# An attention-and-MLP kernel whose static order is planned anew: a policy per stretch, two more result buffers, another first stage

## The chip, the cores and the metric

The kernel runs on one core of one Trainium2 chip. The metric is the device time of one execution in microseconds (us). Before the change it is 673.41 us, the median of three runs (673.37 to 673.63). Engines are named as the profile names them: PE is the matmul engine and PEld its weight loads, ACT the engine of activation functions, DVE the vector engine, POOL the engine beside it, SP the one that issues most DMAs.

## The reference

The input is x of 2048 rows by 512 columns. It is normalized by rows, xn. Two branches read xn and are added to x: attention with 32 heads of 16, and a token-mixing MLP, which normalizes once more and multiplies along the rows.

```python
def _A_ref(x, wqkv, wo):
    H = 32; Dh = D // H
    qkv = (x @ wqkv).reshape(B, S, 3, H, Dh).transpose(2, 0, 3, 1, 4)
    q, k, v = qkv[0], qkv[1], qkv[2]
    scores = jnp.einsum("bhqd,bhkd->bhqk", q, k) * Dh ** -0.5
    p = _softmax(scores, axis=-1)
    o = jnp.einsum("bhqk,bhkd->bhqd", p, v)
    return o.transpose(0, 2, 1, 3).reshape(B, S, D) @ wo

def _B_ref(x, w1, b1, w2, b2):
    h = _layernorm(x, axis=-1)
    u = _gelu(jnp.einsum("bsd,sf->bdf", h, w1) + b1)
    y = jnp.einsum("bdf,fs->bds", u, w2) + b2
    return y.transpose(0, 2, 1)

xn = _layernorm(A_x, axis=-1)
return A_x + _A_ref(xn, A_wqkv, A_wo) + _B_ref(xn, B_w1, B_b1, B_w2, B_b2)
```

Most of the work is the softmax numerator: 32 heads x 2048 x 2048 exponentials.

## The kernel before

**Tiling.** Attention goes in 32 blocks: 4 blocks of 512 queries times 8 groups of 4 heads. In each block the keys go in 16 tiles of 128, so there are 512 groups of one key tile, four heads and 512 queries. A group has four score tiles of 128 x 512 (`score_mm`, L590), one PSUM bank each; the four matmuls use different rows of PE. PSUM has eight banks: 0 to 3 are two pairs for ACT, 6 gathers the products of the block (PV), and 4, 5 and 7 serve everything else.

**Two ways to an exponential.** A group goes to ACT or to the vector side.

- ACT: two exponentials of 128 x 1024 (`exp_tile`, L598), each reading a pair of banks and writing one of eight buffers of the tile pT. PV (`pv_mm`, L610) then needs one set of four matmuls for the group.
- Vector side: the exponential is approximated by writing bit patterns. DVE turns each score bank into 16-bit integers (`dve_first`, L657; `dve_first2` takes two banks at once), which read as bfloat16 are a rough power of two. Two more "planes", the same integers plus a shift, correct it: made by DVE (`add_plane`, L670) or by POOL (`add_plane_pool`, L677). All three planes are multiplied with V, so PV needs three sets of four matmuls. Planes are put wherever memory is free: in the tiles plx, x_sb, xn_sb, h_sb, w1blk, wqkv_sb and xnT once their first contents are done with.

**The first stage** loads x, normalizes the first four row tiles (statistics on DVE at L462 and L466, epsilon and power at L478 and L480 on POOL, the normalization on ACT at L487 for tile 0 and on DVE at L496 for the others), transposes them over PE (L692), copies them to xnT and makes the first Q and K (`qt0_mm`, `k_mm`, L531; `qt_evac`, L551; `k_evac`, L527). After it a dispatcher takes over.

**The order.** All instructions are written out in Python by a planner, class `Sched`: each operation has a planned duration, `add` computes its start from what it depends on, and a loop of `pe_step`, `dve_step` and `misc_step` picks the next operation of each engine at the planned time. On the chip each engine only follows its written order, in order, and waits on semaphores. When ACT's pair of banks is free by the plan, `pe_step` issues two scores for it and one exponential (L598), and as many scores for the vector side as banks are free; otherwise `pe_fill` puts in PV sets or steps of other chains: Q, K and V of later heads (L531), the MLP's two products (L924 and L955, with the Gelu on ACT at L946 between them), the output product (L965). A plan-time rule keeps DVE's planes behind a running POOL plane (`wide`); a POOL operation waits on the chip for the DVE plane ahead of it (`two`).

The choices are steered by 16 numbers, `POLICY`, for instance the lateness that PE may bring to ACT (TOL), when POOL takes a plane (POOL_MIN), when DVE's planes go ahead of its first copies (PL_PRI), and a seed for small variations (SEED). They can differ for each stretch of 10 us of planned time (SEG); before, one row holds for all.

Of the kernel before, what the change touches and what calls it, by code (L numbers as in the profile page):

```python
# [11 lines left out]
F32 = mybir.dt.float32  # L12
# [47 lines left out]
NPB = 8  # L60
NQS = 4
# [34 lines left out]
POLICY = [(150.0, 200.0, 450.0, -1, 0, 1300.0, 0.0, 0.05, 2, 3, 2, 7500.0, 0, 0.0, 1100.0, 0)]  # L96
# [3 lines left out]
POOL_PLANE = 2350.0  # L100
# [173 lines left out]
def bass_parallel_sum__softmax_full_mha__mixer_token_mlp__prompt_kernel(  # L274
# [18 lines left out]
    with ExitStack() as es:  # L293
# [41 lines left out]
        mhalf = sb("mhalf", [128, NT], F32)  # L335
        shift_w = sb("shift_w", [128, NPL], I32)
# [47 lines left out]
        sc.add("pool", lambda e: e.memset(mhalf[:], -0.5), writes=[("mhalf",)], occ=60, lat=130)  # L384
        v17_views = []
# [42 lines left out]
        ld_x(4, 6, 4500)  # L428
        ld_w(2, 0, 1, 5000, "sp")
        ld_x(6, 8, 5500)  # L430
        ld_x(8, 12, 9500)
        ld_x(12, 16, 12500)
# [40 lines left out]
        def ln_stats2(t):  # L473
            if t == NPRE - 1:
# [9 lines left out]
        def ln_norm_act(t):  # L484
            sc.add("pool", lambda e: e.tensor_scalar(r2[:, t:t + 1], mv[:, t, 0:1], mv[:, t, 2:3], -1.0, ALU.mult, ALU.mult),
                   reads=[("mv", t), ("mvr", t)], writes=[("r2",)], occ=230, lat=310)
            return sc.add("act", lambda e: e.activation(xn_sb[:, t, :], x_sb[:, t, :], ACTF.Identity, bias=r2[:, t:t + 1],  # L487
# [99 lines left out]
        def score_mm(g, r, bk, last):  # L587
# [6 lines left out]
                reads=[("KTt", T, kt), ("QT", slot_q), ("QTr", slot_q, r)] + ([("QTh", b)] if b < 2 else []), writes=[("bank", bk)], name="sc",  # L594
                occ=(222.0 if last else 4.0), lat=430.0, cfg="S")

        def exp_tile(slot, buf):
            return sc.add("act", lambda e: e.activation(pT[:, buf, :], ps[:, slot * 1024:(slot + 1) * 1024],  # L598
                                                        ACTF.Exp, scale=EXP_SCALE),
                          reads=[("bank", 2 * slot), ("bank", 2 * slot + 1)], writes=[("pT", buf)], name="exp",  # L600
                          occ=917.0, lat=1080.0)
# [30 lines left out]
        for reg, nm in ((x_flat, "x"), (xn_flat, "xn")):  # L632
            for j in range(4):
# [109 lines left out]
        ln_norm_act(0)  # L743
        ln_stats(1)
# [9 lines left out]
        qt0_mm(0, QB)  # L754
        k_mm(0, KB, 0)
# [1248 lines left out]
```

## Time and profile before

| what | value |
|---|---|
| median of three runs | 673.41 us |
| profiled execution | 673.31 us |
| its span, first to last instruction | 671.5 us |
| ACT busy | 658.0 us, 98% |
| PE busy | 643.1 us, 96% |
| DVE busy | 615.8 us, 92% |
| POOL busy | 355.6 us, 53% |
| exponentials on ACT | 700 |
| PE clock granted | 1.000 |

A line of the profile's groups has the source line, engine and operation, what it writes and reads with the shape, the count, the busy time and the mean duration in ns, then the idle time before it and what ended it. In the timeline a line has its start and its length in us and how many equal instructions follow each other. Busy matmuls are pipelined, so PE's share is not its load.

### The profile page before, as it was taken

To read this page: it belongs to the slowest core of one execution; us is meant where nothing else is said; L and a number is where in the kernel's file an instruction comes from. 1 tells how busy PE (TensorE), PEld (TensorE's weight loads), DVE (VectorE), ACT (ScalarE), POOL (GpSimd) and SP (SyncE) were. 2 spreads that over 40 slices of the span, in tenths; PEclk is the share of its full clock that TensorE was granted. 3 is DMA by queue.
4 is the path that set the end of the run, shared out by engine and by line. 5 is a ranking of instruction groups with operands and counts; after the bars stand their busy time and mean duration, and the time that the engine had idled before them with its cause. 6 is when DMAs were issued, how large, how long until landed. Compare 5 with 4: busy or idle time off the path is not lost.

```text
span 671.5 us, 15513 instructions
## 1 busy us (share of the span) xinstructions
PE 643.1 (96%) x6272; PEld 196.0 (29%) x6348; DVE 615.8 (92%) x1066; ACT 658.0 (98%) x716; POOL 355.6 (53%) x254
## 2 busy tenths in 40 slices
PE   8999999999999999999999999999998999999997
PEld 4533333322222222222222222222222222222222
DVE  7888999999999998999999899999999988999996
ACT  6999999999999999999999999999999999999996
POOL 5620665356465466446655445565645666455570
PEclk9999999999999999999999999999999999999999
DMA  7142100122212222210022121221120222222001
GB/s 220 33 83 42 34 16 17 26 52 51 54 25 44 50 57 53 52 37 19 27 61 53 45 51 45 56 50 34 47 59 20 58 62 49 58 55 52 26 22 48
DMA packets 78368, 32.67 MB, mean 49 GB/s; under 512 B 63004, under 2 KB 74204, under 8 KB 78296
## 3 DMA queue, kind: packets, MB, share of 16 engines
q1 hardware_dynamic: 77864, 31.27, 19.5%
q8 instruction: 50, 0.82, 0.5%
q10 hardware_dynamic: 432, 0.39, 0.2%
q14 instruction: 22, 0.18, 0.1%
HBM read 26.08 MB, written 2.61 MB: 43 GB/s over the span
## 4 chain that ended last, share of the span: by engine, by line
PE 60%; ACT 31%; DVE 6%; issue 1%; DMA 1%; POOL 0%; DVEq 0%
ACT pT L598 30%; PE ps L590 22%; PE ps L610 22%; PE ps L924 6%; PE ps L531 5%; PE ps L955 3%; PE ps L965 1%; DVE plx L657 1%; DVE xn_sb L657 1%; ACT gT L946 1%; DVE x_sb L657 1%; DVE stats L462 1%; DMA den_s<-den_scr 0%; PE ps L692 0%; DVE KT L527 0%
## 5 line engine op out<-in xcount | busy, mean ns | idle before, releaser
L598 ACT ACTIVATE pT<-ps 128x1024 bf16<-128x1024 f32 x700 | 644.1, 1117 | 2.1 <-PE ps L590 1.4
L590 PE MATMUL ps<-QT,KT 32*128 32x512 bf16 x2048 | 283.7, 384 | 10.0 <-ACT pT L598 7.0
L590 PEld LDWEIGHTS ps<-QT,KT 32*128 32x128 bf16 x2048 | 73.8, 91 | 266.5 <-ACT pT L598 245.7
L610 PE MATMUL ps<-pT,V 128*32 128x512 bf16 x1400 | 137.9, 390 | 1.6 <-issue 0.5
L657 DVE TENSOR_SCALAR xn_sb<-ps 128x512 int16<-128x512 f32 x160 | 105.7, 683 | 11.7 <-PE ps L590 10.2
L657 DVE TENSOR_SCALAR x_sb<-ps 128x512 int16<-128x512 f32 x160 | 106.7, 684 | 9.8 <-PE ps L590 8.1
L657 DVE TENSOR_SCALAR plx<-ps 128x512 int16<-128x512 f32 x116 | 76.7, 683 | 6.2 <-PE ps L590 5.9
L610 PEld LDWEIGHTS ps<-pT,V 128*32 128x32 bf16 x1400 | 35.4, 93 | 77.6 <-issue 71.1
L657 DVE TENSOR_SCALAR wqkv_sb<-ps 128x512 int16<-128x512 f32 x80 | 52.8, 684 | 4.0 <-PE ps L590 3.6
L677 POOL TENSOR_TENSOR x_sb<-xn_sb,shift_w 128x1024 int32<-128x1024 int32 x14 | 26.5, 1891 | 51.1 <-DVE x_sb L670 32.7
L924 PE MATMUL ps<-h_sb,w1blk 128*128 128x512 bf16 (+1 forms) x161 | 50.6, 386 | 2.4 <-issue 2.4
L955 PE MATMUL ps<-gT,w2blk 128*128 128x512 bf16 (+1 forms) x151 | 48.9, 384 | 3.3 <-issue 3.2
L531 PE MATMUL ps<-xnT,wqkv_sb 128*128 128x512 bf16 (+1 forms) x166 | 36.0, 305 | 3.8 <-issue 2.7
L657 DVE TENSOR_SCALAR w1blk<-ps 128x512 int16<-128x512 f32 x48 | 31.8, 683 | 2.9 <-PE ps L590 2.3
L610 PE MATMUL ps<-xn_sb,V 128*32 128x512 bf16 x344 | 33.0, 382 | 0.1
L1213 POOL TENSOR_TENSOR oT<-OT,denb 128x512 bf16<-128x512 f32 x16 | 20.3, 1271 | 23.4 <-DVE xn_sb L670 9.4
L657 DVE TENSOR_SCALAR xnT<-ps 128x512 int16<-128x512 f32 x44 | 29.2, 685 | 3.4 <-PE ps L590 3.3
L610 PE MATMUL ps<-x_sb,V 128*32 128x512 bf16 x328 | 31.5, 383 | 0.0
L657 DVE TENSOR_SCALAR h_sb<-ps 128x512 int16<-128x512 f32 x40 | 26.3, 684 | 2.2 <-PE ps L590 2.0
L1213 POOL TENSOR_TENSOR otmp<-OT,denb 128x512 bf16<-128x512 f32 x15 | 19.1, 1271 | 11.5 <-DVE x_sb L670 5.7
L677 POOL TENSOR_TENSOR x_sb<-plx,shift_w 128x1024 int32<-128x1024 int32 x9 | 17.0, 1891 | 14.2 <-DVE x_sb L670 4.4
L677 POOL TENSOR_TENSOR xn_sb<-plx,shift_w 128x1024 int32<-128x1024 int32 x9 | 17.0, 1891 | 12.2 <-DVE xnT L670 4.9
(184 smaller groups left out, 802.7 us busy)
## 6 DMA issues: line engine op xcount, KB each, us to landing
denb<-rec_scr SPq DMA_DIRECT2D x124, 64.0 KB, 2.1
w1blk<-in_B_w_dram SPq DMA_DIRECT2D x10, 512.0 KB, 4.1
w2blk<-in_B_w_dram SPq DMA_DIRECT2D x16, 320.0 KB, 3.4
xres<-in_A_x_dram SPq DMA_DIRECT2D x16, 128.0 KB, 2.9
QT<-qst SPq DMA_DIRECT2D x120, 16.0 KB, 1.8
out_dram<-osb SPq DMA_DIRECT2D x14, 128.0 KB, 1.7
wqkv_sb<-in_A_wqkv_dram SPq DMA_DIRECT2D x3, 384.0 KB, 8.6
x_sb<-in_A_x_dram SPq DMA_DIRECT2D x2, 512.0 KB, 7.9
```

What stands on the lines that cost most here:

```text
L462: return sc.add("dve", lambda e: e.bn_stats(stats[:, t, :], x_sb[:, t, :]), reads=[("x", t)], writes=[("stats", t)], occ=620, lat=725)
L531: return sc.add("pe", lambda e: e.matmul(dst, lhsT=lhsT, rhs=rhs, start=(ct == 0), stop=(ct == NCT - 1)), reads=reads, writes=[("bank", bk ...
L590: return sc.add("pe", lambda e: e.matmul(bank(bk), lhsT=KT[32 * r:32 * r + 32, T, 128 * kt:128 * (kt + 1)], rhs=QT[32 * r:32 * r + 32, slo ...
L598: return sc.add("act", lambda e: e.activation(pT[:, buf, :], ps[:, slot * 1024:(slot + 1) * 1024], ACTF.Exp, scale=EXP_SCALE), reads=[("ba ...
L610: return sc.add("pe", lambda e: e.matmul(bank(PV_BANK)[32 * r:32 * r + 32, :], lhsT=vt_[:, off:off + 32], rhs=rhs, start=start, stop=stop, ...
L657: return sc.add("dve", lambda e: e.tensor_scalar(plane_i[pb][:, 512 * r:512 * (r + 1)], bank(bk), BIAS, 0.0, ALU.add, ALU.max), reads=[("b ...
L677: return sc.add("pool", lambda e: e.tensor_tensor(plane_w[pb], plane_w[pb0], shift_w[:, j:j + 1].broadcast_to([128, 1024]), ALU.add), read ...
L924: op = sc.add("pe", lambda e: e.matmul(bank(xb)[0:m, :], lhsT=w1blk[:, slot, st, 0:m], rhs=h_sb[:, st, :], start=(st == 0), stop=(st == NT ...
L946: op = sc.add("act", lambda e, m=m, f0=f0, f1=f1: e.activation(gT[0:m, f0:f1, :], gT[0:m, f0:f1, :], ACTF.Gelu_apprx_tanh), reads=[("gT", ...
L955: op = sc.add("pe", lambda e: e.matmul(bank(xb), lhsT=w2blk[0:m, slot, ft, :], rhs=gT[0:m, ft, :], start=first, stop=last), reads=([("w2bl ...
L965: return sc.add("pe", lambda e: e.matmul(bank(bk), lhsT=oT[:, par, T, 128 * sti:128 * (sti + 1)], rhs=wo_c[:, T, :], start=first, stop=las ...
L1213: op = sc.add("pool", lambda e: e.tensor_tensor(dst, OT32[:, eb, :], denb[:, :], ALU.mult), reads=[("OT32", eb)] + [("denb", r) for r in r ...
```

## The change

The change has these parts.

1. `POLICY` has 65 rows, one for each 10 us of planned time, for one row before.
2. `POOL_PLANE`, the planned duration of a plane on POOL, is 1888 ns for 2350.
3. ACT may write its exponentials to two further buffers besides the eight of pT (`NPX`). They lie in the last quarter of xn_sb and are used only after the second normalization has read it; one plane less is kept there.
4. In the first stage, Q of the first four tiles goes over banks 7, 4 and 5, for 7 and 4 before; Q is evacuated to QT in pieces of 256, 128 and 128 columns (before 384 and 128); K of tile 1 is made and evacuated there, so that the later chain `k1` holds tiles 2 and 3 alone, for 1 to 3 before; transposes and products of the first tiles are issued in another order; the epsilon of row tile 1 is added by ACT.
5. The planned landing times of x are shorter, and `v_ones(1)` is a step of the dispatcher.

The change was described as an order searched per stretch with three plane makers; in the instructions, planes are made by DVE and POOL before and after.

In the order that comes out, the instructions count as follows.

| instructions | before | after |
|---|---|---|
| exponentials on ACT (128 x 1024) | 700 | 690, five of them into xn_sb |
| first copies on DVE, 128 x 512 | 648 | 658 |
| first copies on DVE, 128 x 1024 | 0 | 5 |
| planes on DVE | 170 | 147 |
| planes on POOL | 154 | 187 |
| PV matmuls | 3344 | 3384 |
| score matmuls | 2048 | 2048 |
| exponentials ahead of the Gelu | 344 | 342 |

On SP, eight row transfers to QT stand ahead of the loads of wo, w1 and w2, which stood ahead of them before.

```diff
+NPX = 2
...
-POLICY = [(150.0, 200.0, 450.0, -1, 0, 1300.0, 0.0, 0.05, 2, 3, 2, 7500.0, 0, 0.0, 1100.0, 0)]
+POLICY = [
+    (160.0, 150.0, 400.0, -1, 0, 1300.0, 0.0, 0.05, 2, 3, 2, 7500.0, 0, 0.0, 1000.0, 1),
+    (115.0, 150.0, 300.0, -1, 0, 900.0, 100.0, 0.05, 2, 5, 2, 8000.0, 84539, 150.0, 1000.0, 1),
...
+]
...
-POOL_PLANE = 2350.0
+POOL_PLANE = 1888.0
...
-        ld_x(4, 6, 4500)
+        ld_x(4, 6, 4100)
...
-            if t == NPRE - 1:
+            if t == 1:
+                sc.add("act", lambda e: e.activation(mv[:, t, 3:4], mv[:, t, 1:2], ACTF.Identity, bias=epsc[:, 0:1]),
+                       reads=[("mv", t), ("epsc",)], writes=[("mve", t)], occ=150, lat=290)
+            elif t == NPRE - 1:
...
+        def pT_buf(buf):
+            return pT[:, buf, :] if buf < NPB else xn_flat[:, 8192 - 1024 * (buf - NPB + 1):8192 - 1024 * (buf - NPB)]
...
-                for j in range(4):
+                for j in range(4 if nm == "x" else 4 - NPX // 2):
...
-        ln_norm_act(0)
-        ln_stats(1)
+        ln_stats1(1)
+        ln_norm_act(0, lambda: ln_stats2(1))
...
-        qt0_mm(0, QB)
-        k_mm(0, KB, 0)
         transpose_mm(2, 0, 0)
         ln_norm(3)
         v_ones(0)
         xnT_evac(2, 1, 0, 0, "dve")
+        qt0_mm(0, QB)
+        k_mm(0, KB, 0)
+        transpose_mm(3, 1, 0)
+        k_evac(0, 1, KB, 0, "act")
+        xnT_evac(3, 1, 1, 0, "dve")
         qt0_mm(1, QB)
-        k_evac(0, 1, KB, 0, "act")
-        transpose_mm(3, 1, 0)
-        xnT_evac(3, 1, 1, 0, "dve")
-        qt0_mm(2, QB)
-        qt0_mm(3, 4)
-        qt_evac(0, QB, "act", 0, 384)
-        qt_evac(0, 4, "act", 384, 512, "QTh")
-        qt_evac(1, 4, "act", 384, 512, "QTh")
-        qt_evac(1, QB, "act", 0, 384)
+        qt_evac(0, QB, "act", 0, 256)
+        qt_evac(1, QB, "act", 0, 256)
+        qt0_mm(2, 4)
+        k_mm(1, KB, 1)
+        qt0_mm(3, 5)
+        k_evac(1, 1, KB, 1)
+        qt_evac(0, 4, "act", 256, 384, "QTh")
+        qt_evac(0, 5, "act", 384, 512, "QTi")
+        qt_evac(1, 4, "act", 256, 384, "QTh")
+        qt_evac(1, 5, "act", 384, 512, "QTi")
         ln_stats(NPRE)
         ln_stats1(NPRE + 1)
-        v_ones(1)
...
-            c = Chain("k1", [Step("pe", lambda t=t: k_mm(t, 5, t - 1), 226) for t in (1, 2, 3)]
-                      + [Step("dve", kdone, 470, frees=True)], due, -1.0, bk=[5])
+            c = Chain("k1", [Step("pe", lambda t=t: k_mm(t, 5, t - 2), 226) for t in (2, 3)]
+                      + [Step("dve", kdone, 340, frees=True)], due, -1.0, bk=[5])
...
-                free_buf = [k for k in range(NPB) if k not in buf_busy]
+                free_buf = [k for k in range(NPB if ln2_left[0] else NPB + NPX) if k not in buf_busy]
```

More of the change, by code (lines that the diff above doesn't have):

```diff
@@ L384, in bass_parallel_sum__softmax_full_mha__mixer_token_mlp__prompt_kernel @@
         sc.add("pool", lambda e: e.memset(mhalf[:], -0.5), writes=[("mhalf",)], occ=60, lat=130)
+        sc.add("pool", lambda e: e.memset(epsc[:], EPS), writes=[("epsc",)], occ=60, lat=130)
         v17_views = []
@@ L427, in bass_parallel_sum__softmax_full_mha__mixer_token_mlp__prompt_kernel @@
                occ=1500)
-        ld_x(4, 6, 4500)
+        ld_x(4, 6, 4100)
         ld_w(2, 0, 1, 5000, "sp")
-        ld_x(6, 8, 5500)
-        ld_x(8, 12, 9500)
-        ld_x(12, 16, 12500)
+        ld_x(6, 8, 4400)
+        ld_x(8, 12, 8400)
+        ld_x(12, 16, 9500)
         ld_w(1, 1, 4, 16000, "sp")
@@ L1273, in bass_parallel_sum__softmax_full_mha__mixer_token_mlp__prompt_kernel @@
             bg.append(chain_ln2(t, 1.5 + 1.0 * t / NT))
-        for i in (2, 3):
+        for i in (1, 2, 3):
             bg.append(Chain("ones%d" % i, [Step("pool", lambda i=i: v_ones(i), gate=lambda i=i: 4 * i + 1 in ln1_done)], -1.0, 0.0))
@@ L1590, in pe_fill @@
             f_first = vary(3) > 0.6
-            pv_press = len(buf_busy) >= NPB - PRESS or len(planes_avail()) < PRESS
+            pv_press = len(buf_busy) >= (NPB if ln2_left[0] else NPB + NPX) - PRESS or len(planes_avail()) < PRESS
             for c in cands:
```

26 lines of the change are left out of this document (19 added, 7 removed), and 63 rows, old and new, of the table POLICY.

## The prediction

> **What bounds the kernel now.** I read the page first: busy shares, the chain that ended last, the costliest group.
>
> ```profile
> span 671.5 us, 15513 instructions
> PE 643.1 (96%) x6272; PEld 196.0 (29%) x6348; DVE 615.8 (92%) x1066; ACT 658.0 (98%) x716; POOL 355.6 (53%) x254
> ...
> PE 60%; ACT 31%; DVE 6%; issue 1%; DMA 1%; POOL 0%; DVEq 0%
> ...
> L598 ACT ACTIVATE pT<-ps 128x1024 bf16<-128x1024 f32 x700 | 644.1, 1117 | 2.1 <-PE ps L590 1.4
> ```
>
> The page's columns: busy time, share, instructions; in the last row 644.1 us busy, 1117 ns for one, 2.1 us idle before them. Three engines look full and the chain gives PE 60%. Which of them sets the pace is told by the waits, read second:
>
> ```profile
> PEld ps L590 <- ACT pT L598: 245.7, 616, 0.8
> ```
>
> ```profile
> ACT pT L598 <- PE ps L590: 1.4, 4, 0.7
> ```
>
> The score matmuls (L590) stand 245.7 us, 616 times, until an exponential of ACT (L598) has read its two banks; ACT stands 1.4 us for the scores. So ACT is the bound from its first exponential to its last, and PE's 96% and its share of the chain are two engines handing the same path to and fro. The third view is ACT's timeline, with one stretch of the chain:
>
> ```profile
> 8.98 1.61 ACT L551 ACTIVATE QT<-ps,qmask 128x384 bf16<-128x384 f32 x4 [0.91 <-PE ps L531]
> 10.47 1.95 ACT L598 ACTIVATE pT<-ps 128x1024 bf16<-128x1024 f32 x2
> 13.06 278.76 ACT L598 ACTIVATE pT<-ps 128x1024 bf16<-128x1024 f32 x302 [0.65 <-PE ps L590]
> ...
> 328.97 1.28 ACT L946 ACT_TABLE_LOAD   x1
> ...
> 336.55 47.87 ACT L598 ACTIVATE pT<-ps 128x1024 bf16<-128x1024 f32 x52
> ...
> 386.03 278.25 ACT L598 ACTIVATE pT<-ps 128x1024 bf16<-128x1024 f32 x303 [0.39 <-PE ps L590]
> 667.29 1.08 ACT L525 ACTIVATE osb<-ps 128x512 bf16<-128x512 f32 x2 [3.01 <-PE ps L973]
> ```
>
> ```profile
> 400.90 123.88 ACT pT L598 x135
> ```
>
> An exponential takes 1.117 us, but the next starts before it ends: 135 in 123.88 us are 0.9176 us apart. The first starts at 10.47, the last ends at 386.03 + 278.25 = 664.28: 653.8 us. 700 x 0.9176 = 642.3, the Gelu with its two table loads 336.55 - 328.97 = 7.6, and 1.12 - 0.92 = 0.2 for the last one's drain make 650.1. So ACT lost 3.7 us in all. Of that, 13.06 - 10.47 - 2 x 0.918 = 0.75 lies before the third exponential. The stretch of 302 ran at (278.76 - 1.12)/301 = 0.9224, so 1.4 more. What is left, about 1.5, is spread out. Ahead lie 10.5 us, behind 671.5 - 664.3 = 7.2.
>
> The time before the first exponential plus their number at 0.9176, plus stalls, plus 7.2: this is the sum I change. The profiled execution took 673.31, of which 671.5 are span and 1.8 lie around it; the median is 673.41, so the sum made against the one moves by 0.1 to the other.
>
> **The change: the count.** The program's order has 690 exponentials after (685 into pT, 5 into xn_sb) for 700 before: five groups of keys, each two exponentials, are computed on the vector side instead (167 groups for 162). 10 x 0.9176 = **-9.18 us**, wholly on the path as long as ACT stays fed. Each gives work to others; their prices:
>
> ```profile
> 455.06 2.47 DVE L657 TENSOR_SCALAR plx<-ps 128x512 int16<-128x512 f32 x4
> ```
>
> ```profile
> L657 DVE TENSOR_SCALAR x_sb<-ps x160: 627/684/692, 85.5 to 649.8; 128x512 int16<-128x512 f32 x160
> ```
>
> ```profile
> L670 DVE TENSOR_SCALAR x_sb<-xn_sb x12: 630/683/694, 65.8 to 636.2; 128x2048 int16<-128x2048 int16 x12
> ```
>
> ```profile
> L677 POOL TENSOR_TENSOR x_sb<-xn_sb,shift_w x14: 1890/1891/1892, 66.6 to 534.1; 128x1024 int32<-128x1024 int32 x14
> ```
>
> ```profile
> 655.49 0.40 PE L610 MATMUL ps<-pT,V 128*32 128x512 bf16 x4
> ...
> 655.72 0.39 PE L610 MATMUL ps<-h_sb,V 128*32 128x512 bf16 x4
> ```
>
> - DVE: 20 more first copies of 512, (2.47 - 0.68)/3 = 0.60 us apart: +12.0. Planes fall from 170 to 147; one has the same length as a copy (0.68), so 0.60 in a row: -13.8. Five pairs of copies become one of 1024 columns, a form not seen before on this line: at worst two copies (0), at best one for two (-3.0); I take 0, the nearer row being the copy itself. DVE comes out 2 to 5 us lighter in 615.8.
> - POOL: planes rise from 154 to 187, 33 x 1.891 = +62.4, so 418 of some 661 us, 63%. It has room, and nothing waits for POOL but PV matmuls and the POOL operations behind.
> - PE: 5 groups leave five PV sets and bring fifteen: 10 more sets of four, 655.72 - 655.49 = 0.23 us each: +2.3. The 245.7 us in which PE waits for ACT hide them; were that cover gone (a set placed in a slot already full), each would put up to 0.23 on ACT.
>
> **Two more result buffers.** Only 5 of 690 exponentials use them. In the trace before no wait for a buffer shows on ACT (its waits are PE's 1.4 us), so I cost this at 0; a buffer wait that stands behind PE's late scores is part of the 1.5 us of scattered loss, which bounds the gain, and a loss is excluded but for 5 extra operands. The word "three plane makers" has no counterpart in the order: planes are made on DVE and POOL alone, as before.
>
> **The first stage.** Rows of the head:
>
> ```profile
> 5.18 0.81 ACT L487 ACTIVATE xn_sb<-x_sb,r,mv 128x512 bf16<-128x512 bf16 x1 [1.29 <-POOL r L485]
> 5.22 0.22 POOL L478 TENSOR_SCALAR mv<-mv 128x1 f32<-128x1 f32 x1
> 5.53 0.57 POOL L480 TENSOR_TENSOR mv<-mv,mhalf 128x1 f32<-128x1 f32 x1
> 6.38 1.25 POOL L480 TENSOR_TENSOR mv<-mv,mhalf 128x1 f32<-128x1 f32 x2
> 7.16 0.93 DVE L496 TENSOR_SCALAR xn_sb<-x_sb,mv 128x512 bf16<-128x512 bf16 x2 [0.46 <-POOL mv L480]
> 8.06 0.94 DVE L527 COPY xnT<-ps 128x512 bf16<-128x512 bf16 x2
> 9.91 0.39 PE L590 MATMUL ps<-QT,KT 32*128 32x512 bf16 x4 [0.46 <-ACT QT L551]
> 10.82 0.71 DVE L496 TENSOR_SCALAR xn_sb<-x_sb,mv 128x512 bf16<-128x512 bf16 x1 [0.21 <-POOL mv L480]
> 11.45 0.67 DVE L462 BATCH_NORM_STATS2 stats<-x_sb 128x6 f32<-128x512 bf16 x1
> 12.04 0.53 DVE L527 CAST KT<-ps 128x384 bf16<-128x384 f32 x1
> 12.63 0.40 PE L590 MATMUL ps<-QT,KT 32*128 32x512 bf16 x4 [0.66 <-DVE KT L527]
> ```
>
> The epsilon of row tile 1 moves from POOL (0.22 at 5.22) to ACT, into its 1.29 us of idleness ahead of the normalization, at 0. A memset of that constant is new on POOL, at most the 0.22 of a small operation there, under the same 1.29. POOL's powers follow each other, so they move up by 5.53 - 5.22 = 0.31, and DVE's norms, which wait 0.46 for them, with them. Q is evacuated in six ACT pieces over banks 7, 4 and 5 instead of four; the two wide ones no longer wait for tiles 2 and 3. That they end sooner is bounded by the 1.61 us of the four; nothing before shows the pieces, so 0 to 0.8. I take **-0.30** for the first exponential: POOL's move alone, as the Q pieces are still behind tile 3's copy (8.06 to 9.00).
>
> The third exponential waited because K tiles 1 to 3 came in one copy at 12.04, behind a norm and statistics on DVE. After, tile 1 has its own copy right behind the xnT copies, about 9.0, and tiles 2 and 3 stand two statistics later, near 11: both ahead of need. So **-0.75** (bounds 0 and -0.75). What is late next: the tiles of row 4 on, whose norms DVE delivers; if they come no sooner, up to 0.4 returns. I take 0.
>
> SP's queue: eight QT row transfers now stand ahead of wo, w1 and w2. Those loads went out before QT at 51.19, and their first reader comes long after:
>
> ```profile
> 43.77 1.82 SPq L367 DMA_DIRECT2D w1blk<-in_B_w_dram  x2
> ...
> 51.19 5.35 SPq L367 DMA_DIRECT2D QT<-qst  x8
> ```
>
> ```profile
> L924 PE MATMUL ps<-h_sb,w1blk x161: 379/380/418, 131.4 to 327.2; 128*128 128x512 bf16 x145, 128*96 128x512 bf16 x16
> ```
>
> 131.4 - 43.8 leaves 87 us against 5.35 of issue: 0. Nothing else of the head stands behind it on SP.
>
> **The searched order.** It is written out anew on every engine; what it does to the 3.0 us of other stalls no row tells: at best all go, -3.0; at worst they double: a run paced throughout like the stretch of 302 loses 690 x 0.0048 = 3.3, about what is lost now, and as much again would be +3.3. Below nothing and above are both open, since the order decides; I take 0, the rate that this scheduler's order shows. The tail keeps its steps: PV, transpose, last wo products, stores: 0.
>
> Sum: -9.18 - 0.30 - 0.75 = -10.2; 673.31 - 10.2 = 663.1, against the median 663.2.
>
> [...] A plane on DVE can meet one on POOL. The planner counts 1888 ns for a POOL plane now and 2350 before; 1891 is measured. So DVE planes used to be set some 459 ns behind POOL's end, and now at it, and any jitter makes them meet. One meeting:
>
> ```profile
> 388.14 1.89 POOL L677 TENSOR_TENSOR wqkv_sb<-xn_sb,shift_w 128x1024 int32<-128x1024 int32 x1 [6.36 <-DVE xn_sb L657]
> ```
>
> ```profile
> 389.77 0.81 DVE L670 TENSOR_SCALAR xnT<-xn_sb 128x2048 int16<-128x2048 int16 x1
> ```
>
> The DVE plane, 0.26 us ahead of POOL's end at 390.03, took 0.81 for 0.68: +0.13, and POOL nothing. If all 147 meet so, 19 us of DVE, in 671.5 - 615.8 = 56 idle: hidden, price 0. [...]
>
> **The rivals.**
> 1. All stalls go. For it: POOL's price in the planner is now the measured one. Against: 3.0 us in 650 is little to find, and spread over hundreds of slots. 663.2 - 3.0 = 660.2; with the Q pieces' upper bound over what I took, 0.5, it is 659.7.
> 2. Slower: DVE planes meet POOL's anywhere in them. POOL holds 187 x 1.891 = 354 of 650 us, 54%; 147 x 0.54 = 79 meetings at half a plane, 0.95, are 75 us, 19 above DVE's 56 idle. PE issues in order, so a bank that DVE frees late holds the scores for ACT too: 663.2 + 19 = 682. It decides from (56 + 10)/79 = 0.84 us a meeting. Against: the one shown cost 0.13, and the 12 planes of a row above lie within 0.63 and 0.69.
> 3. Stalls eat part: PV sets fall in full slots. Stalls doubled (+3.3), no gain at the head (+1.05) and late K tiles (+0.4) give 663.2 + 4.8 = 668.0. For it: ten sets more for ten slots fewer. Against: PE's 245.7 us of waiting. The whole gain lost, 10.2 us or 15 ns an exponential, would be no change.
>
> **How the numbers follow.** Forecast (stalls within 3 us of today's) 0.60; rival 1 0.16; rival 3 0.11, no change 0.04; rival 2 and its smaller kin 0.09. The time is the forecast's, 663.2. The range reaches from rival 1's end to rival 3's, 659.7 to 668.0, and leaves out no change, rival 2 and a little on both sides, about 0.18. 0.2% (1.3 us) is about what a measurement can tell: faster 0.87, same 0.04, slower 0.09.
>
> **What would show it.** 690 exponentials, 0.917 to 0.922 us apart; the first near 10.2 us and no gap before the third; DVE planes 0.63 to 0.82 us; PE still waiting some 240 us for ACT. The forecast is wrong if exponentials stand more than 0.925 us apart over hundreds of them, if DVE's planes take over 1 us by the dozen, or if copies of K hold the scores for the third to the thirtieth exponential.

## The result, and the profile after

The changed kernel takes **664.7 us**, median of four runs (664.15 to 666.23), for 673.39 (673.15 to 673.63) of the kernel before on the same chip: a ratio of 0.9875, 95% interval 0.9857 to 0.9892. In a second set of runs it took 665.0 (662.92 to 665.71), 0.9872 [0.9855, 0.9889]. Its profiled execution took 664.15. The page of it:

```profile
span 662.4 us, 15718 instructions
PE 650.1 (98%) x6387; PEld 191.4 (29%) x6387; DVE 614.1 (93%) x1059; ACT 648.7 (98%) x709; POOL 416.2 (63%) x287
...
PE 72%; ACT 21%; DVE 4%; DMA 1%; SPq 1%; POOL 0%; issue 0%; DVEq 0%; POOLq 0%
...
L686 ACT ACTIVATE pT<-ps 128x1024 bf16<-128x1024 f32 x685 | 630.4, 1133 | 3.2 <-PE ps L663 3.0
L663 PE MATMUL ps<-QT,KT 32*128 32x512 bf16 x2048 | 279.4, 385 | 4.9 <-ACT pT L686 2.9
L663 PEld LDWEIGHTS ps<-QT,KT 32*128 32x128 bf16 x2048 | 71.5, 91 | 269.2 <-ACT pT L686 247.6
```

With five more exponentials into xn_sb ACT does 690. The line numbers have moved: scores L590 to L663, exponentials L598 to L686, DVE's planes L670 to L759, POOL's L677 to L766, the products of Q, K and V L531 to L604, their copies out of PSUM L527 to L600, DVE's first copies L657 to L746, PV L610 to L699, the small copy that will matter L457 to L526. ACT's timeline after:

```profile
8.54 1.87 ACT L624 ACTIVATE QT<-ps,qmask 128x256 bf16<-128x256 f32 x6 [0.17 <-PE ps L604]
10.38 34.15 ACT L686 ACTIVATE pT<-ps 128x1024 bf16<-128x1024 f32 x37
45.51 1.02 ACT L686 ACTIVATE pT<-ps 128x1024 bf16<-128x1024 f32 x1 [0.98 <-PE ps L663]
47.04 1.02 ACT L686 ACTIVATE pT<-ps 128x1024 bf16<-128x1024 f32 x1 [0.50 <-PE ps L663]
48.97 1.02 ACT L686 ACTIVATE pT<-ps 128x1024 bf16<-128x1024 f32 x1 [0.91 <-PE ps L663]
50.23 277.21 ACT L686 ACTIVATE pT<-ps 128x1024 bf16<-128x1024 f32 x302 [0.24 <-PE ps L663]
...
448.42 116.81 ACT L686 ACTIVATE pT<-ps 128x1024 bf16<-128x1024 f32 x127 [0.41 <-PE ps L663]
...
565.79 89.55 ACT L686 ACTIVATE pT<-ps 128x1024 bf16<-128x1024 f32 x97
658.14 1.08 ACT L598 ACTIVATE osb<-ps 128x512 bf16<-128x512 f32 x2 [2.81 <-PE ps L1065]
```

The same sum as in the prediction: the first exponential starts at 10.38, the last ends at 565.79 + 89.55 = 655.34, so 644.96 lie between. 690 x 0.9176 = 633.14, Gelu and drain 7.78, so ACT lost 4.0 us, where it lost 3.7 before. But the loss lies elsewhere. The gap ahead of the third exponential is gone; the long stretch of 302 runs at (277.21 - 1.12)/301 = 0.9172 for 0.9224; and at 45 to 50 us there is a new hole, which was not there before: 50.23 - 10.38 - 40 x 0.9176 = 3.15 us.

| term | us |
|---|---|
| ten exponentials fewer | -9.18 |
| first exponential, 10.47 to 10.38 | -0.09 |
| gap ahead of the third | -0.75 |
| scattered loss, 2.96 to 0.89 | -2.07 |
| new hole at 45 to 50 us | +3.15 |
| tail, 7.22 to 7.06 | -0.16 |
| sum; the spans differ by 671.5 - 662.4 = 9.1 | -9.10 |

The hole begins on VectorE. First a line of the kernel before, then POOL, DVE and PE's weight loads after:

```profile
40.96 0.17 DVE L457 CAST b1h<-b1c_bf 128x11 f32<-128x11 bf16 x1
```

```profile
41.96 3.74 POOL L766 TENSOR_TENSOR x_sb<-plx,shift_w 128x1024 int32<-128x1024 int32 x2
```

```profile
42.25 1.63 DVE L526 CAST b1h<-b1c_bf 128x11 f32<-128x11 bf16 x1
43.79 0.68 DVE L600 CAST V<-ps 128x512 bf16<-128x512 f32 x1
```

```profile
44.52 0.45 PEld L604 LDWEIGHTS ps<-wqkv_sb,xnT 128*128 128x128 bf16 x8 [1.18 <-DVE V L600]
```

A copy of 11 columns, the bias b1h, took 0.17 us before and 1.63 after. It starts in the first of two POOL planes that run on end, and ends with it (42.25 + 1.63 = 43.88 against 41.96 + 1.89 = 43.85). Behind it in DVE's order stands the copy that frees a bank of V, behind that PE's products, and behind those the scores for ACT. The planner keeps DVE's planes away from a running POOL plane; this copy it takes for an ordinary one. The granted clock then adds to it. A table by stretches (start and end, length in us, then busy time and instructions of PE, PEld, DVE, ACT, POOL, then the clock, DMA share and GB/s) of the same execution:

```profile
44.00:46.00 2.00, 1.22 (x11) 0.64 (x11) 2.00 (x4) 1.02 (x2) 1.70 (x1) 1.00 0.75 227
46.00:50.00 4.00, 4.00 (x29) 1.42 (x28) 2.86 (x8) 2.58 (x3) 0.00 (x0) 0.57 0.57 139
```

Behind the pause PE had 0.57 of its clock for four microseconds, and three more exponentials came late.

### The profile page after: what moved, and what is told of

Read it like the earlier page. It is cut to its first block, busy times and chain, and to the rows that moved or that the text cites. A ratio compares the mean times of both kernels' runs of the same rounds, so it can differ in the third digit from the quotient of the medians.

```text
span 662.4 us, 15718 instructions
## 1 busy us (share of the span) xinstructions
PE 650.1 (98%) x6387; PEld 191.4 (29%) x6387; DVE 614.1 (93%) x1059; ACT 648.7 (98%) x709; POOL 416.2 (63%) x287
## 4 chain that ended last, share of the span: by engine, by line
PE 72%; ACT 21%; DVE 4%; DMA 1%; SPq 1%; POOL 0%; issue 0%; DVEq 0%; POOLq 0%
PE ps L663 26%; PE ps L699 26%; ACT pT L686 21%; PE ps L1016 7%; PE ps L604 6%; PE ps L1047 5%; PE ps L1057 2%; SPq L435 1%; PE ps L781 1%; DMA den_s<-den_scr 0%; DVE plx L746 0%; DVE wqkv_sb L746 0%; DMA x_sb<-in_A_x_dram 0%; DVE h_sb L590 0%; ACT QT L624 0%
## 5 line engine op out<-in xcount | busy, mean ns | idle before, releaser
L686 ACT ACTIVATE pT<-ps 128x1024 bf16<-128x1024 f32 x685 | 630.4, 1133 | 3.2 <-PE ps L663 3.0
L663 PE MATMUL ps<-QT,KT 32*128 32x512 bf16 x2048 | 279.4, 385 | 4.9 <-ACT pT L686 2.9
L663 PEld LDWEIGHTS ps<-QT,KT 32*128 32x128 bf16 x2048 | 71.5, 91 | 269.2 <-ACT pT L686 247.6
L699 PE MATMUL ps<-pT,V 128*32 128x512 bf16 x1370 | 129.4, 390 | 0.3 <-DVE OT L1268 0.3
L746 DVE TENSOR_SCALAR x_sb<-ps 128x512 int16<-128x512 f32 x174 | 115.5, 684 | 7.1 <-PE ps L663 6.2
L746 DVE TENSOR_SCALAR xn_sb<-ps 128x512 int16<-128x512 f32 x156 | 102.5, 683 | 6.2 <-PE ps L663 5.5
L746 DVE TENSOR_SCALAR plx<-ps 128x512 int16<-128x512 f32 x106 | 70.2, 684 | 7.6 <-PE ps L663 6.8
L746 DVE TENSOR_SCALAR wqkv_sb<-ps 128x512 int16<-128x512 f32 x78 | 51.3, 684 | 3.9 <-PE ps L663 3.5
L1047 PE MATMUL ps<-gT,w2blk 128*128 128x512 bf16 (+1 forms) x176 | 53.7, 385 | 0.0
L699 PEld LDWEIGHTS ps<-pT,V 128*32 128x32 bf16 x1370 | 32.2, 94 | 67.5 <-issue 63.5
L746 DVE TENSOR_SCALAR xnT<-ps 128x512 int16<-128x512 f32 x64 | 41.9, 682 | 1.9 <-PE ps L663 1.5
L604 PE MATMUL ps<-xnT,wqkv_sb 128*128 128x512 bf16 (+1 forms) x188 | 40.9, 316 | 0.3
L766 POOL TENSOR_TENSOR plx<-xn_sb,shift_w 128x1024 int32<-128x1024 int32 x12 | 22.7, 1891 | 25.4 <-DVE x_sb L759 20.7
L766 POOL TENSOR_TENSOR xn_sb<-x_sb,shift_w 128x1024 int32<-128x1024 int32 x15 | 28.3, 1891 | 15.4 <-DVE xn_sb L759 7.3
L699 PE MATMUL ps<-x_sb,V 128*32 128x512 bf16 x372 | 36.1, 382 | 0.2 <-DVE OT L1268 0.2
L766 POOL TENSOR_TENSOR x_sb<-plx,shift_w 128x1024 int32<-128x1024 int32 x13 | 24.5, 1891 | 13.4 <-DVE x_sb L759 12.1
L746 DVE TENSOR_SCALAR w1blk<-ps 128x512 int16<-128x512 f32 x46 | 30.6, 684 | 1.8 <-PE ps L663 1.3
L766 POOL TENSOR_TENSOR x_sb<-xn_sb,shift_w 128x1024 int32<-128x1024 int32 x12 | 22.7, 1891 | 14.4 <-DVE xnT L759 8.2
L699 PE MATMUL ps<-xn_sb,V 128*32 128x512 bf16 x318 | 30.5, 382 | 0.0
```

The costliest lines, as they stand in the source:

```text
L604: return sc.add("pe", lambda e: e.matmul(dst, lhsT=lhsT, rhs=rhs, start=(ct == 0), stop=(ct == NCT - 1)), reads=reads, writes=[("bank", bk ...
L663: return sc.add("pe", lambda e: e.matmul(bank(bk), lhsT=KT[32 * r:32 * r + 32, T, 128 * kt:128 * (kt + 1)], rhs=QT[32 * r:32 * r + 32, slo ...
L686: return sc.add("act", lambda e: e.activation(pT_buf(buf), ps[:, slot * 1024:(slot + 1) * 1024], ACTF.Exp, scale=EXP_SCALE), reads=[("bank ...
L699: return sc.add("pe", lambda e: e.matmul(bank(PV_BANK)[32 * r:32 * r + 32, :], lhsT=vt_[:, off:off + 32], rhs=rhs, start=start, stop=stop, ...
L746: return sc.add("dve", lambda e: e.tensor_scalar(plane_i[pb][:, 512 * r:512 * (r + 1)], bank(bk), BIAS, 0.0, ALU.add, ALU.max), reads=[("b ...
L766: return sc.add("pool", lambda e: e.tensor_tensor(plane_w[pb], plane_w[pb0], shift_w[:, j:j + 1].broadcast_to([128, 1024]), ALU.add), read ...
```

## The experiments

**The copy that a POOL plane holds.** In the changed kernel the copy goes twelve DVE instructions earlier, where no POOL plane runs. All else keeps its place.

```diff
             sc.add("dve", lambda e: e.tensor_copy(b1h[:], b1c_bf[:]), reads=[("b1c",), ("b1c2",)],
-                   writes=[("b1h",)], occ=80)
+                   writes=[("b1h",)], occ=80, name="b1h")
...
+            z = sc.streams["dve"]
+            i = next(k for k, o in enumerate(z) if o.name == "b1h")
+            o = z.pop(i)
+            z.insert(i - 12, o)
...
         sc.plan()
```

> The changed kernel with one instruction moved: DVE's small copy of b1 to float32 (128 x 11, which took 1.63 us at 42.25 while POOL ran two planes from 41.96 to 45.7) stands 12 instructions earlier on DVE, at about 37.4, where POOL makes no plane. Every other instruction keeps its place. Theory A: that copy was held until POOL's first plane ended, DVE came 1.46 us late, PE waited and its granted clock fell to 0.57, and ACT lost 0.98 + 0.50 + 0.91 + 0.24 = 2.6 us of idle time (3.1 us by the distances of the exponentials). Then the copy takes about 0.17 us, no exponential between 40 and 50 us waits, the clock stays at 1.00 and the time is 664.7 - 3.1 = 661.6, between 661.0 and 662.3, with a smaller spread between runs. Rival B: the loads that now go out at 43 to 50 us (wo, w1, w2 behind the QT rows) hold PE's operands or the K and V copies; then the copy's place changes nothing: 664.2 to 666.2. Rival C: PE's clock falls by itself at this point; the time stays above 663.5 and the clock is still below 1.

Measured: 662.81 us (661.76 to 665.66), 0.985 [0.9826, 0.9874]; the profiled execution 661.76. Its DVE, POOL and ACT:

```profile
37.49 0.16 DVE L526 CAST b1h<-b1c_bf 128x11 f32<-128x11 bf16 x1
```

```profile
42.12 3.75 POOL L766 TENSOR_TENSOR x_sb<-plx,shift_w 128x1024 int32<-128x1024 int32 x2
```

```profile
10.48 314.25 ACT L686 ACTIVATE pT<-ps 128x1024 bf16<-128x1024 f32 x342
```

The copy takes 0.16, the two POOL planes run as before, and the first 342 exponentials are one unbroken run: the hole is gone, and with it 2.4 us of the profiled execution. Rival B, the loads, is out. The median fell by 1.9 us, where theory A expected 3.1, and lies outside its 661.0 to 662.3; the spread, which was expected to shrink, did not. Of rival C something is left: two of the four executions still had a mean clock of 0.994 and 0.997.

The counterpart in the kernel before: the same copy moved four instructions later, into a POOL plane.

```diff
+            z = sc.streams["dve"]
+            i = next(k for k, o in enumerate(z) if o.name == "b1h")
+            o = z.pop(i)
+            z.insert(i + 4, o)
```

> The kernel before with the same small copy moved 4 instructions later on DVE, from 40.96 to about 43.4 us, inside the POOL plane that runs from 43.00 to 44.89. All else is as before. Theory A: the copy takes about 1.4 us instead of 0.17 as it is held to 44.9; the copies of the products and of the next scores behind it come 1.3 us late, and the time rises by 0.5 to 3 us (674 to 676.5), more if PE's clock falls as well. Rival: a copy of 11 columns does not contend with POOL: 0.17 us and 673.4 as before.

Measured: 674.31 us (673.98 to 674.64), 1.0013 [1.0004, 1.0023], so +1.0 us. DVE and POOL:

```profile
43.47 1.49 DVE L457 CAST b1h<-b1c_bf 128x11 f32<-128x11 bf16 x1
```

```profile
43.04 1.89 POOL L677 TENSOR_TENSOR x_sb<-plx,shift_w 128x1024 int32<-128x1024 int32 x1 [2.82 <-DVE x_sb L670]
```

The copy ended with the plane again, 1.49 for 0.17. So the hold can be made and unmade by place alone. Its price was 1.0 us, with the clock at 1.00 throughout. Two plans shown further down, the one without buffers and the one with the old price, happen to put the copy beside a plane as well: it took 1.63 us in each, and ACT lost 1.6 us there with the clock at 1.00. So of the hole's 3.15 us about half is the hold, and the rest the clock. Smallness alone does not make a copy hang. In the changed kernel's trace 460 copies of 512 columns out of PSUM start inside a POOL plane, and none took over 0.75 us; the copy of V above starts at 43.79, just ahead of the second plane, and at 0.68 us is not held by it. Nor were 21 reciprocals of 16 columns, at 0.24 to 0.26 us each. What was held is this copy from one tile in SBUF, the on-chip memory, to another, and DVE's planes, which also go from tile to tile: one took 2.03 us in the second profile of the changed kernel, for 0.68 otherwise (its row stands in the part on the prediction).

The changed kernel once more and the early copy once more, on one chip.

> The changed kernel as it is, for a level beside the next two. Nothing is left out of the computation. Both theories expect 664.7 us (664.1 to 666.3), as in its four runs so far.

> The changed kernel with VectorE's copy of 11 columns (b1h) twelve VectorE instructions earlier, as in the run with the early copy, now beside the changed kernel itself. Theory A (the copy that GpSimd's plane held is worth the 3.07 us of idle ScalarE at 43 to 50 us, less 0.6 that came back elsewhere): 2.0 to 2.8 us below the changed kernel, so 661.8 to 662.7. Rival B (the place only shifts where TensorE's clock dips, and the median keeps what the dips cost): within 1 us of the changed kernel, 663.7 to 665.7.

Measured: 665.0 (662.92 to 665.71) for the first, 662.44 (662.41 to 663.55), 0.9843 [0.9829, 0.9858], for the second: 2.6 us apart, inside theory A's 2.0 to 2.8. Rival B, under 1 us, is out for the medians. But the 2.6 us are not the hold alone: seven of the eight executions of the changed kernel had a mean clock below 0.999, for four of eight with the early copy, and the one at 0.999 took 662.92, 0.5 to 1.2 above those four. And the stretches of the changed kernel in this execution look different:

```profile
46.00:50.00 4.00, 4.00 (x48) 1.44 (x47) 3.51 (x10) 3.67 (x5) 0.00 (x0) 1.00 0.60 161
...
446.00:448.00 2.00, 1.79 (x15) 0.54 (x19) 2.00 (x4) 1.59 (x2) 2.00 (x2) 0.79 0.16 45
448.00:450.00 2.00, 2.00 (x20) 0.25 (x12) 1.00 (x3) 1.08 (x2) 1.38 (x2) 0.50 0.04 4
```

and ACT's first hole:

```profile
39.79 4.75 ACT L686 ACTIVATE pT<-ps 128x1024 bf16<-128x1024 f32 x5
45.52 1.02 ACT L686 ACTIVATE pT<-ps 128x1024 bf16<-128x1024 f32 x1 [0.98 <-PE ps L663]
46.81 5.83 ACT L686 ACTIVATE pT<-ps 128x1024 bf16<-128x1024 f32 x6 [0.26 <-PE ps L663]
```

At 46 to 50 us the clock did not fall this time, and the hole cost 46.81 - 39.79 - 6 x 0.9176 = 1.5 us for 3.15; at 446 to 450 it fell, and ACT lost 2.1 there. The same order of instructions, in two executions, had its slow clock at two different places. In the early copy's second profile it fell at 444 to 448 as well, and two exponentials waited:

```profile
440.00:444.00 4.00, 3.66 (x32) 0.90 (x29) 3.66 (x7) 4.00 (x5) 4.00 (x3) 1.00 0.13 38
444.00:448.00 4.00, 3.63 (x30) 0.86 (x31) 2.56 (x6) 2.24 (x4) 3.80 (x3) 0.60 0.13 34
```

```profile
445.98 1.02 ACT L686 ACTIVATE pT<-ps 128x1024 bf16<-128x1024 f32 x1 [0.85 <-PE ps L663]
447.92 4.80 ACT L686 ACTIVATE pT<-ps 128x1024 bf16<-128x1024 f32 x5 [0.92 <-PE ps L663]
```

Of the eight executions of the early copy four had a mean clock of 0.999 or 1.0 and four of 0.994 to 0.997, among these the slowest, 663.39, 663.55 and 665.66. So a second theory: where the plan has little for PE to do, the clock may fall behind it, and this is the spread.

**The clock.** First, work put wherever PE had little in the last 3.4 us by the plan; that is how long the clock stayed at half in the changed kernel's first profile, from 46.29 to 49.70.

```diff
+                if o.name == "pv" and o.occ > 100 and id(o) not in pv_last and o.start > 15000.0:
+                    if sum(w for a, w in win[-80:] if a >= o.start - 3413.0) < floor:
+                        q = Op("pe", lambda e: e.matmul(bank(PV_BANK), lhsT=zw[:], rhs=KT[:, 0, 0:512], start=False, stop=False), "zero")
```

> The early copy, and 57 matmuls of zeros (128 rows by 512 columns, added into TensorE's PV bank, where they change no value) behind PV sets at which little TensorE work lay in the 3.4 us before. Theory C (what still separates 661.8 from 663 to 666 between executions is TensorE's clock dipping where its work is thin): every execution at a granted clock of 1.00 and the median 661.4 to 662.2. Rival D (the dips do not come from thin work, or the zeros take slots that scores need: 57 x 0.22 us = 12.5 us of TensorE time): the same spread as the early copy or more, median 662.8 to 668.

Measured: 678.76 us (678.33 to 678.86), 1.0081 [1.0066, 1.0096]. Theory C's clock held (0.999 to 1.0 in all executions, spread 0.5 us), but its price was wrong by 16 us. ACT's waits in it:

```profile
ACT pT L687 <- PE ps L663: 9.5, 28, 1.4
```

By the sum, ACT lost 18.2 us, for 1.6 in the first profile of the early copy, which kept its clock too: 16.6/57 = 0.29 us for each zero, no less than the 0.23 us at which sets of PV, as much work, follow each other. So PE has no room in these 57 places, whatever the 247.6 us say in which its weight loads wait for ACT. On the changed kernel's page above, the row of L663 on PE has 2.9 us of such idleness, the one on PEld 247.6. PE is not busy for 662.4 - 650.1 = 12.3 us of that span, so at least 235 of the 247.6 lie under running matmuls: the weights of the next scores wait while PE works off earlier matmuls.

Next, no work added: two PV sets taken from the full stretch at 437 to 440 and put among the scores at 441 to 444.

```diff
+        def move_pv(first, to):
+            z = sc.streams["pe"]
+            ops = z[first:first + 4]
...
+        move_pv(4300, 4314)
+        move_pv(4289, 4318)
```

> The changed kernel with the early copy, and two PV sets (four matmuls each) taken from the full stretch at 437 to 440 us and put among the scores at 441 to 444 us, where TensorE had one set per score pair instead of two. No matmul is added or left out. Theory C (executions differ because TensorE's clock falls to 0.5 behind the thin stretch at 440 to 446 us in some of them, costing 1.8 to 2.7 us there): granted clock 1.00 in all windows of 444 to 450 us, no ScalarE wait over 0.5 us there, median 661.0 to 661.9, executions within 1.5 us of each other. Rival D (the executions differ for another reason, or the later sets free plane buffers late): median 662.4 or more, spread as with the early copy alone (1.1 to 3.9 us).

Measured: 662.54 us (661.83 to 666.2), 0.9847 [0.9826, 0.9868]. Four executions at clock 1.0 took 661.83 to 662.55; the fifth, the profiled one, had 0.992 and took 666.2. In it:

```profile
440.00:442.00 2.00, 1.36 (x13) 0.32 (x13) 1.51 (x4) 2.00 (x3) 2.00 (x2) 1.00 0.05 4
442.00:444.00 2.00, 1.84 (x15) 0.41 (x11) 1.76 (x3) 1.31 (x2) 2.00 (x2) 0.67 0.24 64
444.00:448.00 4.00, 3.75 (x30) 0.77 (x30) 3.12 (x5) 2.53 (x3) 3.85 (x3) 0.50 0.19 36
```

The full stretch had become the thin one: PE stood idle for a third of 440 to 442 us, and the clock fell right there, 2 us earlier than in the runs above, and for longer. So theory C's forecast failed, since the stretch was moved and not filled, and the median and the spread are those of rival D; but the fall followed the thin work to its new place. One execution in five carries that, so it is a hint.

Last, three matmuls of zeros at the two places where PE waited for DVE in that stretch, and nowhere else.

```diff
+        def add_zero(at, n):
...
+                q = Op("pe", lambda e: e.matmul(bank(PV_BANK), lhsT=zw[:], rhs=KT[:, 0, 0:512], start=False, stop=False), "zero")
...
+        add_zero(4318, 1)
+        add_zero(4314, 2)
```

> The changed kernel with the early copy, and three matmuls of zeros (128 rows by 512 columns into the PV bank, where they change no value) among the scores at 441 to 443 us, at the two places where TensorE waited 0.32 and 0.15 us for VectorE; everything else as with the early copy, of whose eight executions four stood at a granted clock of 0.994 to 0.997. Theory C (the clock falls behind the thin stretch of TensorE work at 440 to 446 us): all executions at 0.999 or 1.0 and within 1.5 us of each other, median 661.8 to 662.9 (the zeros cost nothing where TensorE waited, 3 x 0.28 = 0.8 us where it did not). Rival D (work put there does not hold the clock): about half of the executions at 0.994 to 0.997 again, spread 1.1 to 4 us, median 662.4 to 663.5.

Measured: **662.50 us (662.31 to 662.63)**, 0.9838 [0.9824, 0.9851]. All five executions stand at 0.999 or 1.0, and the spread is 0.3 us. Its stretches and ACT:

```profile
440.00:444.00 4.00, 3.69 (x31) 1.02 (x29) 3.80 (x7) 3.64 (x5) 4.00 (x3) 1.00 0.20 45
444.00:448.00 4.00, 3.53 (x48) 0.97 (x44) 3.67 (x7) 3.77 (x5) 3.90 (x3) 1.00 0.14 27
```

```profile
443.61 1.99 ACT L686 ACTIVATE pT<-ps 128x1024 bf16<-128x1024 f32 x2 [0.36 <-PE ps L663]
445.77 6.69 ACT L686 ACTIVATE pT<-ps 128x1024 bf16<-128x1024 f32 x7 [0.17 <-PE ps L663]
```

ACT loses 0.9 us there, for 2.2 in the execution with the fall. Had half the executions kept falling, five at full clock would come once in 32. The median is that of the early copy (662.44 and 662.81), so what the zeros buy is that executions of 663.4 to 665.7 us stay away. This kernel beats the one before, and the changed one by 2.2 to 2.5 us.

The traces settle more of theory C. Each keeps the granted clock as stretches with a start and a length. Every fall ahead of the last exponential lasts 3.41 us (in the moved sets three times that, 442.67 to 452.91) and starts a whole number of 3.41 us after the clock first rose in that execution (in the changed kernel's first profile 12 x 3.413 from 5.33 to 46.29). So each of these executions has its own windows of 3.41 us, and the table by stretches can be cut along them, first for the changed kernel's first profile, then for its second:

```profile
42.88:46.29 3.41, 2.28 (x19) 0.93 (x18) 3.41 (x6) 2.43 (x3) 2.82 (x2) 1.00 0.55 168
46.29:49.70 3.41, 3.41 (x26) 1.23 (x22) 2.27 (x6) 2.00 (x3) 0.00 (x0) 0.50 0.48 112
```

```profile
40.97:44.38 3.41, 2.54 (x22) 1.00 (x19) 3.23 (x5) 3.41 (x4) 3.32 (x3) 1.00 0.10 24
443.74:447.15 3.41, 2.89 (x21) 0.69 (x19) 3.41 (x7) 2.98 (x4) 3.41 (x3) 1.00 0.30 77
447.15:450.56 3.41, 3.41 (x28) 0.65 (x26) 2.41 (x4) 2.05 (x2) 2.23 (x2) 0.50 0.03 5
```

In the first profile one window takes in the whole pause at 43.7 to 44.5 us; in the second a boundary at 44.38 splits it, and the clock stays at 1.00 behind it, to fall behind a thinner window at 443.74. The table lists the thinnest windows of all fourteen traces, from 8 us on to 15 us before the end, without those at half clock. Work is counted in matmuls of 128*128 and 512 columns, the largest in the lines (the zeros have this shape); a score or PV matmul, 32*128 or 128*32 in the lines, counts as a quarter, and one that crosses a boundary is divided by time. This weighing is an estimate.

| trace | window from, us | work | clock behind it |
|---|---|---|---|
| early copy, second | 441.35 | 4.9 | 0.50 |
| changed, second | 443.74 | 4.9 | 0.50 |
| one policy row (below) | 507.54 | 5.0 | 0.50 |
| moved sets | 439.26 | 5.1 | 0.50 |
| changed, first | 42.88 | 5.2 | 0.50 |
| 57 zeros | 452.43 | 5.2 | 1.00 |
| kernel before, late copy | 42.07 | 5.6 | 1.00 |
| early copy, first | 439.81 | 6.3 | 1.00 |
| all others | | 6.3 or more | 1.00 |

The five falls stand behind the five thinnest windows. So theory C holds in this form: in these traces the clock fell only behind a whole window with no more than about 5.2 matmuls, an estimated third of it (at the 0.23 us of a PV set, 5.2 x 0.23 = 1.2 of 3.41 us), and the same order fell or not by where its windows lay. Nearer than that the bound is not known: of two windows at 5.2 one was followed by a fall. Three zeros lift a window of 4.9 to at most 7.9; whether each of the five executions needed them is not known. Idle such a window was not: PE counts as busy for 2.28 and 2.89 us in the two above. When the clock comes back is not settled: in the moved sets it stayed at half for three windows.

**The parts of the change.** Five kernels take one part out of the change or put one part alone. The planner plans each anew, so each has its own number of exponentials. The first stage alone, on the kernel before (one policy row, old price, no extra buffers; 702 exponentials):

```diff
-NPX = 2
+NPX = 0
...
-POLICY = [
...
+POLICY = [(150.0, 200.0, 450.0, -1, 0, 1300.0, 0.0, 0.05, 2, 3, 2, 7500.0, 0, 0.0, 1100.0, 0)]
...
-POOL_PLANE = 1888.0
+POOL_PLANE = 2350.0
```

> The changed kernel with the old single policy row, the old planned POOL plane of 2350 ns and no further buffers: what is new is the first stage and its planned landing times. The planner then writes 702 exponentials on ACT. Theory (time follows the count at 0.9176 us, the new first stage gives 0.09 + 0.75 = 0.84): 673.4 + 1.84 - 0.84 = 674.4, within 1.5 for scattered stalls. Rival (the first stage is a gain by itself): 672.6.

Measured: 680.21 us (679.92 to 682.41), 1.0109 [1.0092, 1.0125], 5.8 over the forecast. ACT and POOL at the end:

```profile
657.85 9.27 ACT L620 ACTIVATE pT<-ps 128x1024 bf16<-128x1024 f32 x10 [1.08 <-PE ps L597]
673.94 1.08 ACT L532 ACTIVATE osb<-ps 128x512 bf16<-128x512 f32 x2 [6.82 <-PE ps L999]
```

```profile
670.31 1.26 POOL L1239 TENSOR_TENSOR oT<-OT,denb 128x512 bf16<-128x512 f32 x1 [10.70 <-DMA denb<-rec_scr]
```

The last exponential ends at 667.12, and the output follows 6.82 us after, not 3.0: the division of a late block waits for its denominators. The tail is 11.0 us for 7.2, which is 3.8 of the 5.8; most of the rest is that ACT lost 4.8 us ahead of it, where the forecast leaves 3.0. The tail, which the forecast took over, depends on the order as much as the rest does.

The changed kernel with the old single row, all else kept (700 exponentials):

```diff
-POLICY = [
...
+POLICY = [(150.0, 200.0, 450.0, -1, 0, 1300.0, 0.0, 0.05, 2, 3, 2, 7500.0, 0, 0.0, 1100.0, 0)]
```

> The changed kernel with the old single policy row in place of the 65 (new first stage, two further buffers and the POOL price of 1888 ns stay). The planner writes 700 exponentials, 5 of them into the further buffers, as the changed kernel has. Theory (the count sets the time, and the count is lowered by the searched rows alone): 673.4 - 0.84 = 672.6 with the scattered stalls of before, 670.6 if they shrink to those of the changed kernel, and up to 3 more if a small copy meets a POOL plane here too. Rival (buffers and POOL's price carry the gain): 664 to 667.

Measured: 674.38 us (672.77 to 675.96), 1.0017 [1.0006, 1.0029]: no gain is left, and it is 1.8 over the forecast. ACT lost 5.0 us in it: the small copy meets no plane (0.17 us), but a DVE plane does, at 84.65 (1.62 us), and the clock fell at 510.95.

The changed kernel without the two buffers (704 exponentials):

```diff
-NPX = 2
+NPX = 0
```

> The changed kernel without the two extra result buffers (0 instead of 2), all else the same; the planner with the same searched rows then plans 704 exponentials instead of 690. Theory A (the time follows the number of exponentials): 664.7 + 14 x 0.9176 = 677.5 us, with stalls and tail between 674 and 681. Rival B (ScalarE was waiting for other things anyway and the buffers matter little): 664 to 668.

Measured: 678.79 us (678.59 to 680.24), 1.0089 [1.0073, 1.0106].

The searched rows alone, in the kernel before (706 exponentials):

```diff
-POLICY = [(150.0, 200.0, 450.0, -1, 0, 1300.0, 0.0, 0.05, 2, 3, 2, 7500.0, 0, 0.0, 1100.0, 0)]
+POLICY = [
...
```

> The kernel before with the 65 searched planner rows in place of its one row, and nothing else of the change; the planner then plans 706 exponentials instead of 700. Theory A (time follows the number of exponentials, and the rows fit only the kernel they were searched for): 673.3 + 6 x 0.9176 = 678.8 us, 677 to 682 with stalls and tail. Rival B (the search of the order carries the gain by itself): 664 to 668.

Measured: 681.60 us (681.01 to 682.21), 1.0123 [1.0109, 1.0137].

The changed kernel with the planner's old price of a POOL plane (702 exponentials):

```diff
-POOL_PLANE = 1888.0
+POOL_PLANE = 2350.0
```

> The changed kernel with the planner's old price of a GpSimd plane, 2350 ns instead of 1888, all else the same; the planner then plans 702 exponentials instead of 690. Theory A (count): 664.9 + 12 x 0.9176 = 675.9 us, 673.5 to 679 with stalls and tail. Rival B (the planes take 1.89 us on the chip whatever the price says, so it changes little): 664 to 667.

Measured: 676.38 us (675.88 to 676.88), 1.0048 [1.0033, 1.0063].

| kernel | exponentials | median us | median less 0.9176 each |
|---|---|---|---|
| changed | 690 | 664.7 | 31.6 |
| before | 700 | 673.4 | 31.1 |
| one policy row | 700 | 674.4 | 32.1 |
| old price | 702 | 676.4 | 32.2 |
| first stage alone | 702 | 680.2 | 36.0 |
| no buffers | 704 | 678.8 | 32.8 |
| rows alone | 706 | 681.6 | 33.8 |

All go by the count to within 2.7 us, but for the late tail of the first stage alone. No part of those tried carries the gain: take away the rows, the price or the buffers and the time is that of before or worse. The likely reason, not shown, is that the rows were searched for this one plan and each part shifts it. The new first stage was not taken away by itself, and what a new search would find without one of the parts was not tried.

## Why the prediction was right or wrong

- **The count** was right and is nearly the whole result: 690 exponentials at 0.9176, -9.18 us, where the spans differ by 9.10. The other kernels of the table follow the same price, but for the 2.7 us and the tail named there.
- **The third exponential** was right: -0.75. DVE copies K of tile 1 at 9.0 and of tiles 2 and 3 at 11.1, as worked out:

```profile
8.99 0.29 DVE L600 CAST KT<-ps 128x128 bf16<-128x128 f32 x1 [0.24 <-PE ps L604]
...
11.12 0.42 DVE L600 CAST KT<-ps 128x256 bf16<-128x256 f32 x1 [0.23 <-PE ps L604]
```

- **The first exponential** was mis-sized: -0.09 for -0.30, inside its bounds. POOL's power did move up, but the six pieces of Q on ACT take 1.87 us (8.54 to 10.41), where the four took 1.61, and the first score waits for them, as it did before:

```profile
9.95 0.40 PE L663 MATMUL ps<-QT,KT 32*128 32x512 bf16 x4 [0.75 <-ACT QT L624]
```

- **The searched order** was the step that failed. I took the scattered 3.0 us as unchanged. They fell by 2.07, and a new hole of 3.15 came. The two nearly cancel, so it is luck that the sum came out only 1.1 us off in the profiled execution, and 1.5 on the median: with the hole's cause gone the kernel stands at 662.4 to 662.8. Of rival 1 (all stalls go) two thirds came; of rival 3, stalls of another kind than the PV sets it named.
- **DVE's planes beside POOL's** were rightly priced at 0 for this trace. It has 17 DVE planes that overlap a POOL plane, for 3 before, the longest at 0.90, in this row:

```profile
L759 DVE TENSOR_SCALAR xn_sb<-x_sb x17: 629/685/901, 59.7 to 577.7; 128x2048 int16<-128x2048 int16 x17
```

That was the luck of this one execution. In the second profile of the same kernel a plane met POOL's nearly at its start (488.03 to 489.92), and ACT lost 1.0 us in the two exponentials behind it:

```profile
488.44 2.03 DVE L759 TENSOR_SCALAR plx<-xnT 128x2048 int16<-128x2048 int16 x1
```

It ended 490.47 - 489.92 = 0.55 us behind POOL's plane; so did the one of 0.90 above (522.29 - 521.74), and the one in the prediction (390.58 - 390.03). The second early copy, the moved sets and both kernels with zeros have one of 1.5 to 1.9 us as well. And the forecast looked at planes alone. The copy of 11 columns is another operation that a POOL plane holds, and one with waiters behind it. Rival 2's mechanism was real, at 1.46 us for the copy and up to three planes over 0.95 us in a trace, and not 79 times. Its half a plane added at each meeting, 0.95 us, was an estimate of mine, and no run shows it as a mean: the 17 meetings of this trace added 0.22 at most (0.90 for 0.68), the one in the second profile 1.35.
- **PE's waiting as cover** was a wrong reading. I wrote that the 245.7 us in which PE waits for ACT hide ten more PV sets. They did fit, but because the planner found places. The zeros, at 0.29 us each on the path, show that the number is no free time of PE, at least at their 57 places. "PE and ACT, with ACT first" would have been the bound to write.
- **Two buffers at 0**: the timeline shows no wait ahead of their five exponentials, as forecast, but the plan without them needs 704. The price of a part in a planned order is what the plan does without it, and the trace of before cannot show that.
- **SP's queue, DVE's load, the tail**: 0 each, as forecast (tail -0.16; DVE 614.1 us for 615.8, 1.7 lighter where 2 to 5 were forecast).

## What to carry to other kernels

Read a bound by the pitch of its repeated instruction, here 0.9176 us, and count those instructions in the new order: here that alone was within 0.5 us of the measured difference of 8.7. Then look in the new order for every operation of a kind that has been seen held by another engine, here a DVE copy from one SBUF tile to another beside a POOL plane, the small ones too (1.63 us for 0.17 at 11 columns), and ask who stands behind it. The 247.6 us in which PE's weight loads waited for ACT were not idle time of PE; only the row of the matmuls, with 2.9 us, says that.

## What was not expected of the hardware

- A VectorE copy of 11 columns took 1.63 and 1.49 us beside a GpSimd plane, and 0.16 to 0.17 away from one: it ended with the plane each time. Copies of 512 columns out of PSUM (0.75 us at most) and reciprocals of 16 columns (0.24 to 0.26) ran beside such planes at their usual length.
- In five of the fourteen traces TensorE's granted clock fell to half for 3.41 us, once for 10.24, in the middle of a busy kernel, behind a window of 3.41 us that PE filled to about a third (an estimate, see the table). The windows lay differently in two executions of the changed kernel (boundaries at 46.29 and at 44.38), and the same order fell at 46.29 in one and at 447.15 in the other. Three matmuls put into the thin stretch kept the clock in five of five. In the five traces with a fall ACT lost 1.3 to 5.1 us around it; the early copy's first profile lost 1.1 at 441 to 446 without one.
